# Float16 halves, turned by DMA, for the queries and keys of two of four batches, a sign step on 16-bit words, and a new order

## The chip, the cores and the metric

The kernel runs on one core of one Trainium2 chip. The metric is the time of one execution in microseconds of the device, from launch to the last output; the median of several runs counts. The core has a matrix engine (TensorE, PE; its weight loads are PEld), a vector engine (VectorE, DVE), a scalar engine (ScalarE, ACT), GpSimd (POOL) and a sync engine (SyncE, SP), which issues the transfers here. Each engine works through its own queue in the order of the program; they wait for each other by semaphores.

## The reference

Causal attention over 4 batches, 12 heads, 448 positions and 64 dimensions a head, and behind it a product of gates on the joined heads (1792 rows of 768):

```python
scores = scale * np.matmul(q, k.transpose(0, 1, 3, 2))      # q, k, v: 4 x 12 x 448 x 64, float32
scores = np.where(mask, -1000000000.0, scores)
scores = scores - np.max(scores, axis=-1, keepdims=True)
attn = np.exp(scores)
attn = attn / (np.sum(attn, axis=-1, keepdims=True) + 1e-09)
x = np.matmul(attn, v)                                      # heads joined: 1792 x 768
a = x @ w1                                                  # w1, w2: 768 x 1024, float64
b = x @ w2
h = a * b @ w3                                              # w3: 1024 x 1024
return h @ w_out                                            # w_out: 1024 x 768
```

## The kernel before, in words

**Weights.** The weights come as float64, two 32-bit words a value. `decode` (line 580) makes float32 of them: ScalarE scales the high word and the low word's top bits (L589, L591), DVE shifts the exponent into place (L593) and puts the sign of the high word into the low one (L595, a scalar_tensor_tensor of and and or over all 32-bit words), GpSimd adds the two (L598). There are 40 such steps, 24 of 768 and 16 of 512 columns, all in the first 235 us. w3 and w_out are multiplied to one matrix first, in f32 on PE (L677 turns, L689 products); this product and w1, w2 are then split into two float16 parts, high and remainder, so that later products run as three float16 matmuls (high by high, high by low, low by high).

**Attention.** `pair(p)` (line 439) handles two heads of one batch; there are 24, six to a batch. It loads k and q with 112 rows on partitions (qkr), turns them on PE in f32 (L457, eight turns a pair) and copies them out of PSUM (L461 on ACT or L462 on DVE) into qkt. The first head's 64 dimensions then lie on partitions 0 to 63, the second's on 64 to 127. `scores(u, due)` multiplies q and k in f32: u = 0 to 2 are the first head's row blocks with 128, 256 and 384 columns, u = 3 to 5 the second's (L495), u = 6 the 64 rows of both tails with 448 columns (L493). In a trace each f32 product is two records. The bank of PSUM that a score block takes is one of four named sc. DVE scales, masks and takes the maximum (L499), ACT takes the exponential (L503), the reciprocal of the sum comes from DVE (L510, L513), and the probabilities are split into two float16 parts (L528, L530 or L532, and L535). A DMA with transpose (L403) turns them into pt and ptt; PE multiplies them with the split v (L556, L561); ACT and DVE write the two parts of x (L570, L571, L573). The scale of v, a power of two, comes from squares summed on ACT (`squares`, L355), a sum over partitions on PE against a tile of ones (`root_scale`, L367) and three small steps on DVE (L370 to L375). `scaled` (L381 to L384) and `remainder` (L390) make the parts.

**Gates and output.** `gate(b)` begins with `norms(b)` (L764), then 16 groups of 18 float16 matmuls of 448 columns (L813 to L815). `project(b)` multiplies with the joined matrix (L873 to L875), and SP sends the result out.

**Order.** Nothing is issued in the order of the code. Every step is put into a list with a due time (`prog.add`), the engines that may do it, and an estimated cost. `Program.order` then runs through the list once, before the kernel exists, and gives each free engine the ready step with the earliest due time; what comes out is the fixed order of every engine's queue. All due times hang on the numbers in PLAN. Before, the estimate for a DVE step of over 0.4 us grows by 0.4 of the time in which GpSimd works beside it.

**Memory.** Buffers are rings: two for qkr and qkt, three for p32 and pt, three for da (decoding and squares). Of the 16 tiles w16 with the parts of w1 and w2, nc = 11 lie in fixed memory; the others lie in memory that is free once the f32 product of w3 and w_out is through (the keys w0 and w5).

Of the kernel before, what the change touches and what calls it, by code (L numbers as in the profile page):

```python
# [26 lines left out]
PLAN = dict(nc=11, wstep=2.3205, soft=49.445, w0=118.4, w34=0.5037, ab=1.5277, out=0.179, gap=16.057, lat=37.703, begin=100.181, wlead=94.567, urgent=13.056, flex=96.023, sc=-27.259, vo=62.311, av=-129.283, x=-15.194, qlead=-18.284, rlead=-5.245, v0=30.056, v1=123.832, gram=2, nf=3, h0=3, hv=5, ns=7, wo0=-132.371, wo1=27.123, wom=21.268, w3a=15.279, w3l=17.856, wd=16.165, wh=-60.261, wl=58.537, fin=8.526, ev=-0.539, po=[-24.2, -29.15, -19.26, 10.49, -17.08, -21.38, -42.72, -39.55, -25.07, -1.21, -22.27, 20.91, 0.72, -56.42, -27.16, -10.64, -22.5, -16.12, -21.26, -21.97, -35.13, 2.64, -7.32, 4.13], wo=[-28.62, 5.45, -16.93, 42.18, 23.33, -12.43, 22.11, -20.21], w3=[-35.5, -43.06, -39.69, 7.92, 8.15, -9.78, -9.89, -29.26], tw=[-16.09, -51.07, -16.26, 0.98, -3.04, -29.34, -21.69, -23.59, -23.52, -22.71, -68.85, 16.04, -16.6, -4.06, -30.21, 7.83], slack=0.7, pflex=42.748)  # L27
# [19 lines left out]
class Program:  # L47
# [3 lines left out]
    def __init__(self):  # L51
        self.ops, self.writer, self.readers = [], {}, {}
        self.banks, self.leased, self.first = {}, [], set()

# [31 lines left out]
    def order(self):  # L86
# [12 lines left out]
        dma_free = 0.0  # L99
# [11 lines left out]
        while len(result) < n:  # L111
# [81 lines left out]
def t_pool(n):  # L193
    return (2.1 * n + 150) / 1000
# [7 lines left out]
def tile_causal_attention_moe(ctx: ExitStack, tc: tile.TileContext, q, k, v, w1, w2, w3, wo, out):  # L202
# [33 lines left out]
    def ring(shape, dt, name, n):  # L236
        return Ring(name, fixed(shape, dt, name, n))
# [40 lines left out]
    qkt = ring([P, 2, S], F32, "qkt", 2)  # L278
# [109 lines left out]
    def remainder(dst, src, s, hi, n, due, reads, writes, stage=None):  # L388

        prog.add(due, (DVE, t_dve(n) + 0.06, lambda: nc.vector.scalar_tensor_tensor(  # L390
            out=dst, in0=src, scalar=s, in1=hi, op0=ALU.mult, op1=ALU.subtract)), reads, writes, stage)
# [47 lines left out]
    def pair(p):  # L439
# [10 lines left out]

        qt, qtk = qkt.next()
        for i in (1, 0):
            ps, key = prog.lease("sc", "tr")

            def turn(i=i, ps=ps):
# [5 lines left out]
                (ACT, t_act(S, True), lambda i=i, ps=ps: nc.scalar.copy(out=qt[:, i], in_=ps[:, :S])),  # L461
                (DVE, t_dve(S), lambda i=i, ps=ps: nc.vector.tensor_copy(qt[:, i], ps[:, :S])),  # L462
            ], [key], [qtk + (i,)])

# [17 lines left out]
        def scores(u, due):  # L482
# [6 lines left out]
            def products():  # L489
                for j in range(2):  # L490
                    rows = slice(j * D, (j + 1) * D)
                    if i == 2:
                        nc.tensor.matmul(ps[rows, :w], qt[rows, 0, 3 * P : S], qt[rows, 1, 0:w], start=True, stop=True)  # L493
                    elif i == j:
                        nc.tensor.matmul(ps[:, :w], qt[rows, 0, c * P : (c + 1) * P], qt[rows, 1, 0:w], start=True, stop=True)  # L495

            prog.add(due, (PE, 0.9 if i == 2 else max(2 * t_mm(w) + 0.1, 0.31), products),
                     [qtk + (1,), qtk + (0,)], [key, tk + (c,)] + ([tk] if p < 2 else []))
            prog.add(due + 0.4, (DVE, t_dve(w) + 0.09, lambda: nc.vector.tensor_tensor_reduce(  # L499
                out=o, in0=ps[:, :w], in1=m, scale=minus, scalar=-NEG,  # L500
                op0=ALU.add, op1=ALU.min, accum_out=mx[:, u : u + 1])),
                [key, "minus", "mask_t" if i == 2 else "mask"], [mk + (u,), tk + (c,)] + ([tk] if p < 2 else []))
# [12 lines left out]
        def soft(i, us, due):  # L515
# [3 lines left out]
            for u in reversed(us):  # L519
# [5 lines left out]
                else:  # L525
# [9 lines left out]
                prog.add(due + 0.4, (DVE, t_dve(w) + 0.06, lambda src=src, r=r, h=h, l=l: nc.vector.scalar_tensor_tensor(  # L535
                    out=l, in0=src, scalar=r, in1=h, op0=ALU.mult, op1=ALU.subtract)),
# [5 lines left out]
        for n, u in enumerate((2, 5, 1, 4, 0, 3, 6)):  # L542
            scores(u, T + PLAN["sc"] + 0.3 * n)
# [37 lines left out]
    def decode(raw, rawk, n, due, t=None, tk=None):  # L581
# [11 lines left out]
        prog.add(due + 1, (DVE, t_dve(n, True), lambda: nc.vector.tensor_scalar(  # L593
            out=ai, in0=ai, scalar1=3, scalar2=None, op0=ALU.logical_shift_left)), [ak], [ak])
# [21 lines left out]
    def take_w(i):  # L616
# [19 lines left out]
        prog.add(T + PLAN["wl"], (DVE, t_dve(DM) + 0.06, lambda: nc.vector.scalar_tensor_tensor(  # L636
# [335 lines left out]
```

## Time and profile before

| what | value |
|---|---|
| median of 3 runs | 641.41 us (641.22 to 641.45) |
| the profiled execution, its own time | 642.41 us |
| its span, first to last instruction | 640.6 us |
| PE, DVE, ACT, POOL busy | 601.3, 405.5, 318.7, 175.0 us |
| mean granted clock of PE | 0.974 |
| PE's share of the chain that ended last | 74%, DVE 14%, issue 5% |
| DMA | 78.29 MB, 54.3% of 16 engines' span |
| start of norms for gates 0 to 3 (L764) | 208, 318, 443, 549 us |
| tail scores of pairs 12, 18 and 23 (L493) | 296, 417, 523 us |

A line of the profile names the source line, the engine, the operation and the tiles, then count, busy time and mean. PE is pipelined: the time of one matmul runs on under the next, so what a matmul costs is read from the start of one to the start of the next. The granted clock is a share of full speed; 1.00 is 2.4 GHz, and means between 0.5 and 1 are mixtures of the two levels, 1.2 and 2.4 GHz.

### The profile page before, as it was taken

Reading aid. Unit: us, or ns where it says so; the run is one execution under the profiler, and the core shown is the slowest. Engines: PE = TensorE matmul, PEld = TensorE weight load, DVE = VectorE, ACT = ScalarE, POOL = GpSimd, SP = SyncE. Lnnn points to the kernel's source line nnn. Section 1 sums busy time; section 2 is a strip of 40 time slices with the busy share of each in tenths; the row PEclk is TensorE's granted clock in tenths of the full one; section 3 lists DMA queues with packets and bytes.
Section 4 is the critical chain, followed back from the end, with each engine's and each line's share of the span. In section 5 each row is a group of like instructions: output and inputs, shape, how many; then the busy total and the mean of one; then the engine's idle time right before and its main releaser. Section 6 shows DMA issues by size and latency. Waiting matters only on the chain.

```text
span 640.6 us, 10699 instructions
## 1 busy us (share of the span) xinstructions
PE 601.3 (94%) x3892; PEld 342.3 (53%) x3892; DVE 405.5 (63%) x1048; ACT 318.7 (50%) x739; POOL 175.0 (27%) x129
## 2 busy tenths in 40 slices
PE   3799969987989999999999999999999999999997
PEld 1454545655545555565655556555555556555564
DVE  7966999999989889866543358846528861212200
ACT  7546988587666867446331336635425441111111
POOL 5643754641554524313100023311102210000000
PEclk9899978988889999999999999999999999999999
DMA  8899596464888949759610139797107616000011
GB/s 340 248 235 226 130 235 169 133 186 111 162 153 170 189 103 154 129 102 185 141 30 19 40 76 176 152 172 143 29 2 150 125 23 124 26 1 1 0 50 49
DMA packets 198836, 78.29 MB, mean 122 GB/s; under 512 B 179840, under 2 KB 195712, under 8 KB 198784
## 3 DMA queue, kind: packets, MB, share of 16 engines
q1 hardware_dynamic: 198784, 77.61, 54.3%
q8 instruction: 30, 0.49, 0.3%
q14 instruction: 22, 0.18, 0.1%
HBM read 43.78 MB, written 5.51 MB: 77 GB/s over the span
## 4 chain that ended last, share of the span: by engine, by line
PE 74%; DVE 14%; issue 5%; ACT 4%; DMA 2%; POOL 0%; SPq 0%; DVEq 0%; ACTq 0%; POOLq 0%
PE sc L495 8%; PE mm L813 7%; PE mm L814 7%; PE mm L815 7%; PE mm L873 4%; PE mm L875 4%; PE mm L874 4%; PE mm L689 3%; PE tr L813 3%; PE tr L814 3%; PE tr L815 3%; PE av L561 3%; PE sc L493 3%; PE sc L689 2%; PE sc L457 2%
## 5 line engine op out<-in xcount | busy, mean ns | idle before, releaser
L532 POOL TENSOR_SCALAR ph<-p,rc 128x256 f16<-128x256 f32 (+2 forms) x47 | 52.8, 1128 | 162.2 <-DVE rc L513 66.4
L814 PE MATMUL mm<-xt,w 128*128 128x448 f16 x258 | 91.4, 354 | 1.9 <-DVE xt L573 1.9
L813 PE MATMUL mm<-xt,w 128*128 128x448 f16 x258 | 91.6, 355 | 0.4 <-ACT xt L570 0.2
L815 PE MATMUL mm<-xt,w 128*128 128x448 f16 x258 | 91.6, 355 | 0.0
L503 ACT ACTIVATE p<-p,mx 128x384 f32<-128x384 f32 (+2 forms) x144 | 71.7, 499 | 37.9 <-DVE mx L499 37.7
L499 DVE CUSTOM_DVE_ANT_0 p<-sc,mask,minus 128x384 f32<-128x384 f32 (+2 forms) x144 | 64.0, 480 | 30.6 <-PE sc L495 29.9
L495 PE MATMUL sc<-qkt 64*128 64x384 f32 (+2 forms) x288 | 72.8, 415 | 5.2 <-DVE mx L499 2.7
L689 PE MATMUL mm<-wof,w3t 128*128 128x384 f32 x192 | 73.3, 522 | 3.5 <-POOL wof L598 3.5
L535 DVE SCALAR_TENSOR_TENSOR ph<-p,rc,ph 128x384 f16<-128x384 f32 (+2 forms) x144 | 67.1, 509 | 3.6 <-ACT ph L530 2.3
L495 PEld LDWEIGHTS sc<-qkt 64*128 64x128 f32 x288 | 41.5, 190 | 40.3 <-issue 9.7
L813 PEld LDWEIGHTS <-w 128*128 128x128 f16 x384 | 38.2, 100 | 38.4 <-issue 5.5
L815 PEld LDWEIGHTS <-w 128*128 128x128 f16 x384 | 37.7, 98 | 38.0 <-issue 3.5
L814 PEld LDWEIGHTS <-w 128*128 128x128 f16 x384 | 37.8, 98 | 30.8 <-issue 1.1
L689 PEld LDWEIGHTS mm<-wof,w3t 128*128 128x128 f32 x192 | 36.6, 203 | 25.8 <-issue 4.7
L873 PE MATMUL mm<-w34h,arena 128*128 128x384 f16 x152 | 49.8, 327 | 0.0
L875 PE MATMUL mm<-w34h,arena 128*128 128x384 f16 x152 | 49.5, 326 | 0.0
L874 PE MATMUL mm<-w34l,arena 128*128 128x384 f16 x152 | 49.5, 326 | 0.0
L813 PE MATMUL tr<-xt,w 128*128 128x448 f16 x126 | 44.9, 357 | 0.0
L814 PE MATMUL tr<-xt,w 128*128 128x448 f16 x126 | 44.9, 356 | 0.0
L815 PE MATMUL tr<-xt,w 128*128 128x448 f16 x126 | 44.9, 356 | 0.0
L839 ACT CAST arena<-g 128x448 f16<-128x448 f32 x21 | 11.8, 564 | 57.4 <-DVE g L834 57.3
L834 DVE SCALAR_TENSOR_TENSOR g<-mm,y,at 128x448 f32<-128x448 f32 x17 | 11.6, 684 | 42.0 <-PE mm L815 41.8
(165 smaller groups left out, 1097.6 us busy)
## 6 DMA issues: line engine op xcount, KB each, us to landing
arena<-in_moe_w_dram SPq DMA_DIRECT2D x11, 768.0 KB, 4.7
qkr<-in_k_dram SPq DMA_DIRECT2D x24, 224.0 KB, 4.0
qkr<-in_q_dram SPq DMA_DIRECT2D x24, 224.0 KB, 4.7
vr<-in_v_dram SPq DMA_DIRECT2D x24, 192.0 KB, 4.3
out_dram<-osb SPq DMA_DIRECT2D x24, 192.0 KB, 2.0
arena<-in_moe_w_dram SPq DMA_DIRECT2D x8, 512.0 KB, 4.4
xt<-in_moe_w_dram SPq DMA_DIRECT2D x5, 768.0 KB, 4.7
arena<-in_moe_w_out_dram SPq DMA_DIRECT2D x3, 768.0 KB, 6.7
```

Of the source, the lines that this page charges most:

```text
L495: nc.tensor.matmul(ps[:, :w], qt[rows, 0, c * P : (c + 1) * P], qt[rows, 1, 0:w], start=True, stop=True)
L499: prog.add(due + 0.4, (DVE, t_dve(w) + 0.09, lambda: nc.vector.tensor_tensor_reduce(out=o, in0=ps[:, :w], in1=m, scale=minus, scalar=-NEG, ...
L503: prog.add(due + 0.9, (ACT, t_act(w, pointers=1, acc=True), lambda: nc.scalar.activation(out=o, in_=o, func=AF.Exp, scale=-1.0, bias=mx[:, ...
L532: (POOL, t_pool(w) + 0.35e-3 * w + 0.16, lambda src=src, r=r, h=h: nc.gpsimd.tensor_scalar(out=h, in0=src, scalar1=r, scalar2=None, op0=AL ...
L535: prog.add(due + 0.4, (DVE, t_dve(w) + 0.06, lambda src=src, r=r, h=h, l=l: nc.vector.scalar_tensor_tensor(out=l, in0=src, scalar=r, in1=h ...
L689: prog.add(due, (PE, 4 * t_mm(NH), lambda: nc.tensor.matmul(ps[:, :NH], w3t[slot(m)][:, g], wof[:, g, ns], start=g == 0, stop=g == KF - 1) ...
L813: nc.tensor.matmul(ps[:, :S], w[:, 0, d], xh, start=d == 0, stop=False)
L814: nc.tensor.matmul(ps[:, :S], w[:, 0, d], xl, start=False, stop=False)
L815: nc.tensor.matmul(ps[:, :S], w[:, 1, d], xh, start=False, stop=d == KD - 1)
L873: nc.tensor.matmul(t, gh[:, fc, cs], w34h[:, fc, ns], start=fc == 0, stop=False)
L874: nc.tensor.matmul(t, gh[:, fc, cs], w34l[:, fc, ns], start=False, stop=False)
L875: nc.tensor.matmul(t, gl[:, fc, cs], w34h[:, fc, ns], start=False, stop=fc == KF - 1)
```

## The change

Three things. **First**, the pairs of batches 2 and 3 (b >= PLAN["fq"] = 2) no longer go through PE's f32 turns. `halved` loads q and k in their natural layout (three loads each, 256-byte rows), finds a power of two as a scale for each, as v has one (squares on ACT, a sum on PE, three steps on DVE), splits each into a float16 high part and remainder, and has a DMA turn both parts at once (8 blocks of 128 by 128). The scores of these pairs are three float16 passes, each a step of its own in the list, with due times that put the two heads' passes side by side. The scale goes out again in DVE's step at L499 (scale=iv in place of minus). GpSimd clears the unused rows of the two qkr buffers once. Batches 0 and 1 keep the old way, as `turned_whole`. **Second**, the sign step takes the top 16-bit word of the high word, keeps its top bit and writes it as the top 16-bit word of the low word; the low word's value has three bits, so nothing is lost. **Third**, the estimate of DVE beside GpSimd counts only marked steps, and all numbers of PLAN are new, nc among them (10 for 11).

```diff
@@ Program.order @@
-                if e == DVE and cost > 0.4:
-                    cost += 0.4 * max(0.0, min(free[POOL], t + cost) - t)
+                if e == DVE and emit in self.shared:
+                    cost += 0.9 * max(0.0, min(port, t + cost + 1.0) - t)
+                    port_dve = t + cost
+                if e == POOL and emit in self.pairs:
+                    cost += 0.6 * max(0.0, min(port_dve, t + cost) - t)
+                    port = t + cost
...
+    def halved(p, b, hs, T, qk, qkk, qt, qtk):
+
+        q16 = qt.rearrange("p i f -> p (i f)").bitcast(F16).rearrange("p (i t f) -> p i t f", i=2, t=2)
+        inverse_of = []
+        for i, src in ((1, k), (0, q)):
...
+            squares(am, flat, lambda n16=n16: n16[:, 1].bitcast(BF16), 4 * P, T - PLAN["hlead"], raw_k, [ak, nk])
+            sc_, sck, e, ek = root_scale([am], [ak], "q", T - PLAN["hlead"])
+            inverse_of.append((e, ek))
+            scaled(n16[:, 0], flat, sc_, 4 * P, T - PLAN["hlead"] + 0.5, raw_k + [sck], [nk])
+            remainder(n16[:, 1], flat, sc_, n16[:, 0], 4 * P, T - PLAN["hlead"] + 1, raw_k + [sck, nk], [nk])
+            dma(q16[:, i].rearrange("p t (c f) -> p (t c) f", f=P), n16.rearrange("p t f -> p (t f)"), T - PLAN["hlead"] + 1.5,
+                [nk], [qtk + (i,)], P * P * 2 * 8, turn=True)
...
+        halves = b >= PLAN["fq"]
...
+            if halves:
+                q16 = qt.rearrange("p i f -> p (i f)").bitcast(F16).rearrange("p (i t f) -> p i t f", i=2, t=2)
+                for m_, (a, b_) in enumerate(((0, 0), (0, 1), (1, 0))):
+                    prog.add(due + 0.01 * m_, (PE, t_mm(w) / (1 if i == 2 else 2) + 0.02, lambda a=a, b_=b_, m_=m_: products(
+                        q16[:, 0, a], q16[:, 1, b_], m_ == 0, m_ == 2)),
+                        [qtk + (1,), qtk + (0,)], [key, tk + (c,)] + ([tk] if p < 2 else []))
...
-            scores(u, T + PLAN["sc"] + 0.3 * n)
+            scores(u, T + PLAN["sc"] + 0.3 * (2 * (n // 2) if halves else n) + 0.001 * n)
...
+        parts16 = raw.rearrange("p n t -> p (n t)").bitcast(I16).rearrange("p (n t) -> p n t", t=4)
...
-        prog.add(due + 1, (DVE, t_dve(n) + 0.06, lambda: nc.vector.scalar_tensor_tensor(
-            out=raw[:, :, 0], in0=raw[:, :, 1], scalar=-0x80000000, in1=raw[:, :, 0], op0=ALU.bitwise_and, op1=ALU.bitwise_or)),
+        prog.add(due + 1, (DVE, 0.9 if n > 512 else 0.65, lambda: nc.vector.tensor_scalar(
+            out=parts16[:, :, 1], in0=parts16[:, :, 3], scalar1=-0x8000, scalar2=None, op0=ALU.bitwise_and)),
             rawk + [low], [low])
-        prog.add(due + 2, (POOL, t_pool(n) + 0.2, lambda: nc.gpsimd.tensor_tensor(
-            out=t.bitcast(I32), in0=ai, in1=raw[:, :, 0], op=ALU.add)), rawk + [ak, low], tk)
+        prog.add(due + 2, (POOL, t_pool(n) + 0.1, prog.alone(lambda: nc.gpsimd.tensor_tensor(
+            out=t.bitcast(I32), in0=ai, in1=raw[:, :, 0], op=ALU.add))), rawk + [ak, low], tk)
...
```

## Rows read from the trace of the kernel before

**Rows 1.** The page, busy tenths in 40 slices, PE and DVE

```profile
PE   3799969987989999999999999999999999999997
DVE  7966999999989889866543358846528861212200
```

**Rows 2.** By stage: PE, PEld, DVE, ACT, POOL busy, granted clock, DMA share, GB/s

```profile
0.00:80.00 80.00, 64.98 (x226) 35.16 (x226) 62.29 (x112) 53.14 (x106) 44.22 (x39) 0.98 0.85 235
80.00:160.00 80.00, 68.80 (x283) 42.91 (x282) 74.34 (x150) 61.66 (x116) 37.75 (x20) 0.88 0.59 167
160.00:240.00 80.00, 73.46 (x576) 42.40 (x577) 73.15 (x208) 54.49 (x135) 36.42 (x24) 0.95 0.81 155
...
320.00:440.00 120.00, 119.15 (x858) 66.65 (x857) 64.47 (x197) 49.81 (x136) 21.03 (x18) 1.00 0.51 101
440.00:560.00 120.00, 119.16 (x906) 67.42 (x904) 63.78 (x190) 44.22 (x111) 14.12 (x12) 1.00 0.35 71
```

**Rows 3.** The same table for lines 495, 493, 457 alone (PE, PEld)

```profile
320.00:560.00 240.00, 25.91 (x120) 14.52 (x120) 1.00 0.43 86
...
320.00:560.00 240.00, 9.69 (x40) 1.94 (x40) 1.00 0.43 86
...
320.00:560.00 240.00, 9.97 (x80) 8.61 (x80) 1.00 0.43 86
```

**Rows 4.** PE in order of time: both heads' scores, tail, gate (start, us)

```profile
452.30 1.35 PE L495 MATMUL sc<-qkt 64*128 64x384 f32 x8
453.92 0.48 PE L495 MATMUL sc<-qkt 64*128 64x128 f32 x2 [0.28 <-DVE mx L499]
...
455.43 0.97 PE L493 MATMUL sc<-qkt 64*64 64x448 f32 x4
456.33 0.36 PE L813 MATMUL mm<-xt,w 128*128 128x448 f16 x1
456.53 0.35 PE L814 MATMUL mm<-xt,w 128*128 128x448 f16 x1
```

**Rows 5.** The same view: one head's scores, then value products

```profile
388.56 1.56 PE L495 MATMUL sc<-qkt 64*128 64x384 f32 x6
390.06 0.36 PE L813 MATMUL mm<-xt,w 128*128 128x448 f16 x1
...
392.14 1.15 PE L561 MATMUL av<-pt,v 128*64 128x384 f16 x18
393.22 1.12 PE L495 MATMUL sc<-qkt 64*128 64x384 f32 x3
```

**Rows 6.** The same view: the two sums of v's scale

```profile
475.07 0.50 PE L367 MATMUL sc<-vam,ones 128*128 128x1 f32 x4
475.43 0.35 PE L813 MATMUL mm<-xt,w 128*128 128x448 f16 x1
```

**Rows 7.** Busy DVE by stage, the sign step (line 595) alone

```profile
0.00:80.00 80.00, 32.51 (x21) 0.98 0.85 235
80.00:160.00 80.00, 16.44 (x16) 0.88 0.59 167
160.00:240.00 80.00, 4.20 (x3) 0.95 0.81 155
```

**Rows 8.** One line's DVE instructions: ns min/median/max, first and last start

```profile
L595 DVE SCALAR_TENSOR_TENSOR arena<-arena x22: 680/948/2591, 5.7 to 230.4; 128x768 int32<-128x768 int32 x14, 128x512 int32<-128x512 int32 x8
...
L593 DVE TENSOR_SCALAR da<-da x38: 385/550/2211, 5.2 to 231.4; 128x768 int32<-128x768 int32 x24, 128x512 int32<-128x512 int32 x14
...
L390 DVE SCALAR_TENSOR_TENSOR v<-vr,v_s,v x24: 736/746/992, 153.9 to 524.8; 128x512 f16<-128x512 f32 x24
```

**Rows 9.** PE's waits by line up to 250 us: total, times, longest

```profile
PE sc L367 <- ACT w L355: 7.0, 4, 2.7
```

**Rows 10.** The tail tile's turn by DMA: SP's queue, time to landing

```profile
L403 SPq DMA_TRANSPOSE ptt<-pht x24: 1233/1736/2013, 77.5 to 534.5; - x24
...
DMA to landing us min/median/max: 3.0/3.6/6.0
```

More of the change, by code (lines that the diff above doesn't have):

```diff
@@ L53, in __init__, with beside, alone @@
         self.banks, self.leased, self.first = {}, [], set()
+        self.shared, self.pairs = set(), set()
+    def beside(self, emit):
+        self.shared.add(emit)
+        return emit
+    def alone(self, emit):
+        self.pairs.add(emit)
+        return emit
     def lease(self, *pools):
@@ L388, in remainder @@
     def remainder(dst, src, s, hi, n, due, reads, writes, stage=None):
-        prog.add(due, (DVE, t_dve(n) + 0.06, lambda: nc.vector.scalar_tensor_tensor(
-            out=dst, in0=src, scalar=s, in1=hi, op0=ALU.mult, op1=ALU.subtract)), reads, writes, stage)
+        prog.add(due, (DVE, t_dve(n) + 0.06, prog.beside(lambda: nc.vector.scalar_tensor_tensor(
+            out=dst, in0=src, scalar=s, in1=hi, op0=ALU.mult, op1=ALU.subtract))), reads, writes, stage)
     def less(dst, a, b, n, due, reads, writes):
@@ L437, in tile_causal_attention_moe, with turned_whole, turn @@
     UP = 2.0**14
+    def turned_whole(p, b, hs, T, qk, qkk, qt, qtk):
+        for i, src in ((1, k), (0, q)):
+            dma(qk[0:QP, i], src[b, hs].rearrange("h (p r) d -> p r h d", r=4),
+                T - PLAN["qlead"], (), [qkk + (i,)], 2 * S * D * 4, rate=181e3)
+        for i in (1, 0):
+            ps, key = prog.lease("sc", "tr")
+            def turn(i=i, ps=ps):
+                for r in range(4):
+                    nc.tensor.transpose(ps[:, r:S:4], qk[0:QP, i, r].rearrange("p h d -> p (h d)"), ident[0:QP, 0:QP])
+            prog.add(T + 0.1 * (1 - i), (PE, 4 * t_mm(2 * QP), turn), [qkk + (i,)], [key, qtk + (i,)])
+            prog.add(T + 0.5, [
+                (ACT, t_act(S, True), lambda i=i, ps=ps: nc.scalar.copy(out=qt[:, i, :S], in_=ps[:, :S])),
+                (DVE, t_dve(S), lambda i=i, ps=ps: nc.vector.tensor_copy(qt[:, i, :S], ps[:, :S])),
+            ], [key], [qtk + (i,)])
+        return minus, "minus"
@@ L439, in pair, with clear_pads @@
+    def clear_pads(due):
+        for n, t in enumerate(qk_raw.tiles):
+            kk = ("qkr", n)
+            prog.add(due, (POOL, 0.4, lambda t=t: nc.gpsimd.memset(t[D:P, :, 3], 0.0)), [], [kk + (i, *n) for i in range(2) for n in ((), (0,), (1,), (2,))])
     def pair(p):
@@ L445, in pair @@
         hs = slice(2 * hp, 2 * hp + 2)
[L446 to L448 removed]
+        halves = b >= PLAN["fq"]
         qt, qtk = qkt.next()
[L452 to L463 removed]
+        load = halved if halves else turned_whole
+        iv, ivk = load(p, b, hs, T, qk, qkk, qt, qtk)
         vs, vsk, _, _ = vsc[b]
@@ L487, in scores, with products @@
             m = mask_t if i == 2 else mask[:, (2 - c) * P :]
-            def products():
+            n = min(P, S - c * P)
+            def products(qs, ks, start, stop):
                 for j in range(2):
                     rows = slice(j * D, (j + 1) * D)
[L492 to L495, printed above, removed]
@@ L635, in take_w @@
         ], tk + [sk] + w5, [("w16h", i)])
-        prog.add(T + PLAN["wl"], (DVE, t_dve(DM) + 0.06, lambda: nc.vector.scalar_tensor_tensor(
-            out=w16[i][:, 1], in0=tc2, scalar=s, in1=w16[i][:, 0], op0=ALU.mult, op1=ALU.subtract)),
+        prog.add(T + PLAN["wl"], (DVE, t_dve(DM) + 0.06, prog.beside(lambda: nc.vector.scalar_tensor_tensor(
+            out=w16[i][:, 1], in0=tc2, scalar=s, in1=w16[i][:, 0], op0=ALU.mult, op1=ALU.subtract))),
             tk + [sk, ("w16h", i)] + w5, [("w16l", i)])
```

52 lines of the change are left out of this document (34 added, 18 removed).

## The prediction

> **What bounds the kernel now.** I read the page's row of slices first [rows 1], then the table by stage [rows 2], then what each stage's engines do by line. Two regimes show. From 240 us on, TensorE (PE) has no room: 119.15 of 120 us busy in each of the two late windows, at the full granted clock, while VectorE (DVE) works 64.47 and 63.78 of 120 [rows 2]. There a microsecond of matmul taken away is a microsecond of time, as long as no new wait appears. Before 240 us it is the other way round: between 80 and 240 DVE is busy 74.34 and 73.15 of 80, PE 68.80 and 73.46 of 80, and the granted clock is 0.88 and 0.95, part of it at the lower level, because PE idles [rows 2]. There DVE's load decides more than PE's. The change touches both: float16 scores act on the late stage (batches 2 and 3, pairs 12 to 23, whose tail tiles start at 296 us by the table above), the sign step on the first 240 us, the new order on all.
>
> **Scores of the last two batches: what goes.** The window from 320 to 560 us holds the score work of ten pairs (40 records of L493, four to a pair). In it PE is busy 25.91 us with the six f32 products of 128 to 384 columns (L495), 9.69 us with the tail tile (L493) and 9.97 us with the eight f32 turns (L457) [rows 3]: 4.56 us a pair. A block's last matmul drains under the next block's first (the L493 block counts 0.97 us, but the next matmul starts 0.90 us after it, 455.43 to 456.33 [rows 4]), so I take off 0.25 us for the blocks' ends: 4.3 us a pair go.
>
> **What comes in its place on PE.** (a) The six products in three float16 passes. No float16 score stands in the trace, but the value products have the same columns: three passes of 384, 256 and 128 columns for two heads side by side, 18 matmuls, 392.14 to 393.22, 1.08 us [rows 5]. That is the price if the two heads' products, which stand in different halves of the array's rows, run at the same time; if not, twice that, 2.16 us. (b) The tail tile: three passes of 448 columns, two halves at once, at 0.20 us a step (456.33 to 456.53 [rows 4]), and 0.1 us for the way in and out: 0.7 us. (c) Two sums over partitions, for the scale of q and of k: the v scale's two sums cost 0.36 us (475.07 to 475.43 [rows 6]). (d) A wait for a score bank: only four exist. Where both heads run at once PE already waits 0.28 us for DVE before the 128-column product [rows 4]; the float16 products fill the four banks some 0.4 us earlier, DVE empties them no faster, so I add 0.3 us, and 0 as the other end where the order puts gate matmuls between.
>
> Do the heads run at once? In f32 they do where the order put them beside each other: 384 and 256 columns of both heads take 452.30 to about 453.6, 1.35 us, eight records [rows 4]; one head's 384, 256 and 128 alone take 1.49 us, 388.56 to 390.06 [rows 5]. Blocks of the first kind number seven between 330 and 520 us, so somewhat more than half of the pairs. The new due times put heads 2 and 5, 1 and 4, 0 and 3 within a thousandth of each other, pass by pass, so I take eight of twelve. Paired: 1.08 + 0.7 + 0.36 + 0.3 = 2.4, a saving of 1.9 us; unpaired: 2.16 + 0.7 + 0.36 = 3.2, a saving of 1.1. Eight and four: 19.6 us.
>
> A rule of the Trainium skill speaks against counting on that. Its page "TensorEngine Tiling (Array Packing)", section "Key Properties", says that different tiles run in parallel, but also that changing the tiling mode, not just the tile, drains TensorE. The trace agrees in sign and sizes it: the way into and out of a score block costs about 0.1 us each. By that rule every pass that stands alone among gate matmuls would pay both ways; it is the first rival below.
>
> (e) Waits. The change puts three new things ahead of PE's in-order queue: the sum waits for ScalarE's squares, the scores wait for the turned halves. The only row of such a sum is L367 behind L355: 7.0 us in four waits [rows 9]; over the 28 sums of weights and v in that kernel that is 0.25 us each, and 24 new sums would cost 6 us. Ends 0 and 6; I take 1.5, because those waits fell where ScalarE and DVE were crowded. Behind a waiting sum stand the gate and output matmuls, and behind those everything. Late term: 19.6 - 1.5 = **18 us**, ends 7 (all unpaired, full waits) and 26 (all paired, no bank wait).
>
> **The rest of the float16 path** I cost at nothing, with its cover named. DVE gets two remainders of 512 columns at 0.75 us [rows 8] and seven small operations a pair, about 2.5 us, 30 us for twelve pairs; it loses the few turned-tile copies that fell to it. DVE has about 56 us of 120 free in each late window [rows 2], so it goes from 53% to some 70%: hidden unless it bunches up in front of a score bank. ScalarE loses two copies and gains two squares and up to two scalings; it has more room than DVE. On SP's queue come four more loads and two turns a pair. The nearest row is the turn of the tail tile, of the same size: 1.74 us of SP's queue, 3.6 us to landing, 6.0 at the worst [rows 10]. These pass in front of the probability turns on the same queue; the cover is that q and k have two buffers, so a pair's halves may be made a pair ahead. If that cover is gone, see the slower rival.
>
> **Sign step.** L595 is 32.51, 16.44 and 4.20 us of DVE in the first three windows, 53.2 us for 40 instructions [rows 7], though one takes 0.68 us at the least and 0.95 at the median; the worst took 2.59 [rows 8]: part of it is time lost beside GpSimd. The new operation reads one source and half the bytes. The costs written in the diff are 0.9 us for 768 columns and 0.65 for 512; by them 24 and 16 instructions take 32 us: 21 us less. Ends: the old operation undisturbed, about 0.95 and 0.68, 34 us (19 less), and the trace's one-source shift on tiles of the same width (L593, median 0.55 us [rows 8]), 22 us (31 less). I take 21: 16.4 of it in the first 80 us, 4.8 between 80 and 240. What is that worth in time? In the first 80 us loads, start-up and PE's f32 products limit as well (PE busy 64.98 of 80, DMA share 0.85 [rows 2]), so little comes straight out; in the DVE-bound stretch 4.8 come straight out, and something of the 16.4 if softmax work is pulled forward. Ends 0 and 20 (PE idles about 18 us between 80 and 240, and the low clock hides some more). I take **7 us**.
>
> **Order and tiles.** All due times are new, with a finer price for DVE beside GpSimd. The trace can't price an order; I give it 0 with 5 us either way. One w16 tile fewer lies ahead of the point where the first stage's memory is given back; gate 0 asks for it only after ten groups of 18 matmuls at 0.19 us, some 34 us in, so it costs nothing unless that point slips.
>
> **Sum.** 642.41 us of the profiled execution (span 640.60 and 1.81 around it) less 18 and 7 is 617.4. The median of the runs lies 1.0 us under the profiled one, so the forecast is 616.4 us.
>
> **Rivals.**
> First, the passes scatter: heads unpaired and half of the passes single among gate matmuls. Then a pair saves 1.1 us less about 0.6 for three extra blocks at 0.2: 6 us for twelve pairs; with 4 us early, 632 profiled, 631 us. For: score work is now three program steps per product, each free to be put elsewhere. Against: each pass is ready the moment the one before ends, and the due times differ by hundredths. Chance 0.17.
> Second, the first third is really DVE's: all 20 us of the early end come out, with 21 late: 601 profiled, 600 us. For: DVE at 92% from 80 to 240 [rows 2]. Against: most of the sign step lies before 80 us [rows 7]. Chance 0.13.
> Third, slower: SP's queue. Two turns a pair at 1.74 us each [rows 10] stand in an in-order queue in front of the probability turns and of the next pair's loads. If they pass through to PE, twelve pairs cost 12 x 3.5 = 42 us against 25 saved: 659 us. It decides from 25/12, about 2.1 us of PE wait a pair, and such waits would lower the clock too. For: the turn needs the longest new chain (load, squares, sum, scale, remainder, turn). Against: PE's only wait for such work today is in [rows 9], and queue time of two turns is small against some 20 us a pair. Chance 0.10.
> Fourth, it doesn't do what it says: DVE's added 30 us delay the gate's products, and PE's saved time becomes waits for banks: no change, 641. Chance 0.03.
>
> **How the numbers follow.** Forecast case 0.50 (608 to 624 by its own ends), first rival 0.17 (626 to 638), second 0.13, third 0.10, fourth 0.03; 0.07 for weaker mixtures between 633 and 640. A difference under 0.2%, 1.3 us, can't be told from no change in this kernel. Faster: 0.50 + 0.17 + 0.13 + 0.07 = 0.87; same 0.03; slower 0.10. The range of 602 to 637 leaves out about half of the second rival, the slower ones and a little of the mixtures, 0.2 in all.
>
> **What would show it.** Right: in the late windows PE still above 99% busy; no turns by L457 after the third batch begins; float16 score blocks of both heads near 1.1 us a pair, starts a few ns apart; the last gate's norms (549 us in the table above) some 22 us sooner; L595 near 0.9 and 0.65 us; norms of gate 0 (208 us there) some 7 us sooner. Wrong: PE idle behind the new sums or the new turns, score steps alone between gate matmuls, the clock under 1.00 after 240 us, or a gate 0 that starts no earlier with DVE less busy.

## The result, and the profile after

| | median us | range | against before |
|---|---|---|---|
| before | 641.32 | 638.58 to 641.45 | |
| after | 625.08 | 624.77 to 625.31 | 0.9761 (0.9735 to 0.9786) |

The change takes 16.2 us off, where 25 were forecast; the time lies inside the range. The profiled span went from 640.6 to 623.3 us.

The page of the kernel after: TensorE's (PE's) busy time, then busy tenths of PE and VectorE (DVE) and the granted clock in 40 slices.

```profile
PE 586.3 (94%) x3940; PEld 327.7 (53%) x3940; DVE 428.0 (69%) x1155; ACT 331.2 (53%) x781; POOL 189.4 (30%) x138
...
PE   2999974999989899999999999999999999999997
...
DVE  6977879799999878985666775597697853212100
...
PEclk9999985899999799999999999999999999999999
```

PE has 15.0 us less to do (601.3 before). Its slices stay at 9 from some 218 us on, where they did from some 192 us in [rows 1]; DVE's late slices are fuller. By stage (columns as in [rows 2]):

```profile
0.00:80.00 80.00, 66.28 (x230) 35.24 (x231) 64.67 (x123) 53.20 (x103) 42.04 (x37) 1.00 0.95 248
80.00:160.00 80.00, 66.56 (x293) 40.16 (x293) 70.81 (x143) 58.96 (x113) 45.27 (x25) 0.85 0.64 167
160.00:240.00 80.00, 74.67 (x552) 43.09 (x549) 70.52 (x212) 56.68 (x147) 37.53 (x26) 0.94 0.73 146
320.00:440.00 120.00, 120.00 (x963) 65.99 (x964) 88.65 (x291) 63.56 (x176) 25.32 (x21) 1.00 0.71 133
440.00:545.00 105.00, 105.00 (x850) 58.35 (x849) 65.08 (x200) 45.58 (x118) 16.63 (x14) 1.00 0.51 99
```

Two things are to be seen. In the late stage PE is at 100% and at the full clock, with DVE at 88.65 of 120: the halved path's extra DVE work is hidden. In the first 240 us PE is busy 207.5 us in sum, against 207.2 by [rows 2]: nothing came out there, although DVE is less busy between 80 and 240. The norms of gates 0 to 3 now start at 213.2, 314.4, 430.5 and 531.8 us: gate 0 is 5 us later, the last one 17.2 us sooner. All of the gain arises behind gate 0.

Where it went is told best by PE's time from the start of each matmul to the start of the next, idle time taken out, added up over the whole trace by what is computed. The last three columns belong to experiments told of below.

| PE, us | before | after | halves alone | no halves | halves, two due times |
|---|---|---|---|---|---|
| f32 scores | 91.1 | 52.4 | 49.7 | 91.0 | 51.6 |
| float16 scores | 0 | 25.8 | 27.6 | 0 | 28.4 |
| f32 turns of q, k | 20.5 | 11.8 | 11.9 | 20.7 | 10.6 |
| sums for their scales | 0 | 4.5 | 5.1 | 0 | 4.8 |
| *score path, sum of the four* | 111.6 | 94.6 | 94.3 | 111.7 | 95.4 |
| gates | 224.4 | 223.9 | 227.9 | 223.3 | 226.1 |
| all other matmuls | 265.1 | 267.5 | 265.9 | 266.1 | 266.7 |
| PE stands still | 27.0 | 24.7 | 41.3 | 26.7 | 23.0 |

The score path is 17.0 us shorter, and the span 17.3. The other rows shift by up to 2.5 us either way and nearly cancel.

One pair's scores in the kernel after, PE in order of time (start, us; the counterpart of [rows 4]):

```profile
452.21 0.99 PE L550 MATMUL sc<-qkt 64*128 64x384 f16 x12
453.13 0.36 PE L878 MATMUL mm<-xt,w 128*128 128x448 f16 x1
453.33 0.35 PE L879 MATMUL mm<-xt,w 128*128 128x448 f16 x1
453.52 0.35 PE L880 MATMUL mm<-xt,w 128*128 128x448 f16 x1
453.81 0.34 PE L550 MATMUL sc<-qkt 64*128 64x128 f16 x3
454.08 0.36 PE L878 MATMUL mm<-xt,w 128*128 128x448 f16 x1
...
454.75 1.02 PE L550 MATMUL sc<-qkt 64*128 64x128 f16 x9
455.70 0.36 PE L878 MATMUL mm<-xt,w 128*128 128x448 f16 x1
```

The first block holds 12 matmuls, the 384 and the 256 columns of both heads: the second head's start 3 to 4 ns after the first's, and the next matmul follows 0.92 us after the first. The 128 columns come head by head (0.27 us to the next gate matmul; the last group holds the other head's and the tail). Between them stand gate matmuls, and no float16 score waits for a bank. PE's only wait for another engine after 240 us is this one, at 274 us, in front of an f32 score of the second batch (PE's waits by line: total, times, longest):

```profile
PE sc L550 <- DVE mx L563: 0.3, 1, 0.3
```

The sign step (L660, DVE, the stages of [rows 7]) and its instructions (ns min/median/max):

```profile
0.00:80.00 80.00, 28.22 (x21) 1.00 0.95 248
80.00:160.00 80.00, 16.16 (x17) 0.85 0.64 167
160.00:240.00 80.00, 2.08 (x2) 0.94 0.73 146
...
L660 DVE TENSOR_SCALAR arena<-arena x22: 735/1024/2386, 5.8 to 237.1; 128x768 int16<-128x768 int16 x14, 128x512 int16<-128x512 int16 x8
```

It is 46.5 us for 53.2, not 32, and its median is longer than the old one's, 1024 ns against 948 in [rows 8].

### The profile page after: what moved, and what is told of

It is laid out like the page before. It is cut to its first block, busy times and chain, and to the rows that moved or that the text cites. A ratio compares the mean times of both kernels' runs of the same rounds, so it can differ in the third digit from the quotient of the medians.

```text
span 623.3 us, 11048 instructions
## 1 busy us (share of the span) xinstructions
PE 586.3 (94%) x3940; PEld 327.7 (53%) x3940; DVE 428.0 (69%) x1155; ACT 331.2 (53%) x781; POOL 189.4 (30%) x138
## 4 chain that ended last, share of the span: by engine, by line
PE 82%; DVE 8%; DMA 4%; ACT 3%; issue 2%; POOL 1%; SPq 0%; DVEq 0%; ACTq 0%; POOLq 0%
PE sc L550 11%; PE mm L878 9%; PE mm L879 8%; PE mm L880 8%; PE mm L754 6%; PE mm L938 4%; PE mm L940 4%; PE mm L939 4%; PE av L625 4%; PE tr L878 4%; PE tr L880 4%; PE tr L879 4%; PE tr L938 2%; PE av L620 2%; PE tr L939 2%; PE tr L940 2%
## 5 line engine op out<-in xcount | busy, mean ns | idle before, releaser
L878 PE MATMUL mm<-xt,w 128*128 128x448 f16 x264 | 93.5, 354 | 0.0
L879 PE MATMUL mm<-xt,w 128*128 128x448 f16 x264 | 93.1, 353 | 0.0
L880 PE MATMUL mm<-xt,w 128*128 128x448 f16 x264 | 93.1, 353 | 0.0
L567 ACT ACTIVATE p<-p,mx 128x384 f32<-128x384 f32 (+1 forms) x144 | 71.6, 498 | 31.9 <-DVE mx L563 31.1
L550 PE MATMUL sc<-qkt 64*128 64x384 f16 (+6 forms) x480 | 84.7, 367 | 2.1 <-DVE mx L563 1.9
L599 DVE SCALAR_TENSOR_TENSOR ph<-p,rc,ph 128x384 f16<-128x384 f32 (+2 forms) x144 | 72.6, 546 | 0.2
L879 PEld LDWEIGHTS <-w 128*128 128x128 f16 x384 | 37.6, 98 | 28.7 <-issue 0.6
L938 PE MATMUL mm<-w34h,arena 128*128 128x384 f16 x152 | 49.7, 327 | 0.0
L878 PE MATMUL tr<-xt,w 128*128 128x448 f16 x120 | 42.5, 354 | 0.1
L880 PE MATMUL tr<-xt,w 128*128 128x448 f16 x120 | 42.3, 353 | 0.0
L879 PE MATMUL tr<-xt,w 128*128 128x448 f16 x120 | 42.3, 353 | 0.0
L563 DVE CUSTOM_DVE_ANT_0 p<-sc,mask,minus 128x256 f32<-128x256 f32 (+2 forms) x72 | 33.2, 477 | 12.3 <-PE sc L550 11.9
L550 PEld LDWEIGHTS sc<-qkt 64*128 64x128 f32 (+1 forms) x192 | 24.3, 178 | 25.7 <-issue 9.2
L563 DVE CUSTOM_DVE_ANT_0 p<-sc,mask,qiv 128x384 f32<-128x384 f32 (+2 forms) x72 | 30.9, 480 | 10.0 <-PE sc L550 9.7
```

Of the source, the lines that this page charges most:

```text
L550: nc.tensor.matmul(ps[rows if i == 2 else slice(0, P), :w], qs[rows, c * P : c * P + n], ks[rows, 0:w], start=start, stop=stop)
L567: prog.add(due + 0.9, (ACT, t_act(w, pointers=1, acc=True), lambda: nc.scalar.activation(out=o, in_=o, func=AF.Exp, scale=-1.0, bias=mx[:, ...
L599: prog.add(due + 0.4, (DVE, t_dve(w) + 0.06, prog.beside(lambda src=src, r=r, h=h, l=l: nc.vector.scalar_tensor_tensor(out=l, in0=src, sca ...
L878: nc.tensor.matmul(ps[:, :S], w[:, 0, d], xh, start=d == 0, stop=False)
L879: nc.tensor.matmul(ps[:, :S], w[:, 0, d], xl, start=False, stop=False)
L880: nc.tensor.matmul(ps[:, :S], w[:, 1, d], xh, start=False, stop=d == KD - 1)
```

## Experiments

Ratios are to the kernel before, run on the same chip; 0.001 is 0.64 us. The four of the first group tell the parts apart.

**The sign step alone**: before, with its 16-bit form and the same queues.

```diff
-        ... scalar_tensor_tensor(out=raw[:, :, 0], in0=raw[:, :, 1], scalar=-0x80000000, in1=raw[:, :, 0], ...)
+        ... tensor_scalar(out=parts16[:, :, 1], in0=parts16[:, :, 3], scalar1=-0x8000, ..., op0=ALU.bitwise_and)
```

> The kernel before with the sign step on 16-bit words alone; the planned costs are left as they were, so every engine's queue has the same order. Theory A (the operation itself saves nothing: alone it takes 1.03 us for 768 columns in the changed kernel against 0.95 before, and both stand still behind a two-tensor add of GpSimd that has begun): 641 us, within 1.5, and L595's total stays within 50 to 56 us. Rival B (the 16-bit step gives back its 5 to 7 us of DVE and the new order lost them again): 634 to 637 us.

Measured: 639.94 us, ratio 0.9994 (0.998 to 1.0009). The step takes 53.6 us of DVE for 40 instructions, as before (53.2). Its instructions:

```profile
L596 DVE TENSOR_SCALAR arena<-arena x22: 727/1031/2691, 5.8 to 228.5; 128x768 int16<-128x768 int16 x14, 128x512 int16<-128x512 int16 x8
```

So with the order held fixed the step carries nothing, in DVE time or in the end.

**The old sign step in the new order**: after, with line 660 put back.

```diff
-        ... tensor_scalar(out=parts16[:, :, 1], in0=parts16[:, :, 3], scalar1=-0x8000, ...)
+        ... scalar_tensor_tensor(out=raw[:, :, 0], in0=raw[:, :, 1], scalar=-0x80000000, in1=raw[:, :, 0], ...)
```

> The changed kernel with the old sign step (both 32-bit words, two tensors) under the same planned costs, so the order is that of the changed kernel. Theory A: 625 us, within 1.5, a shade quicker if anything. Rival B: 629 to 632 us, since the changed order would then carry 7 us more of DVE work before 240 us.

Measured: 623.85 us, ratio 0.9756 (0.9731 to 0.978), not told apart from after. The old step took 42.7 us here, less than the new one in the same order. That the total went from 53.2 to 46.5 between before and after is the order's doing: of the 40 instructions, 15 took over 0.6 us more than their time alone in before and 12 with the new step in before's order, but 7 in after and 6 here.

**The halves alone**: before's due times and estimates, with the halved path for batches 2 and 3. The halving's own due time, hlead, is that of the new plan.

```diff
-PLAN = dict(nc=11, ..., pflex=42.748)
+PLAN = dict(nc=11, ..., pflex=42.748, fq=2, hlead=-11.33)
+    def halved(p, b, hs, T, qk, qkk, qt, qtk):
...
```

> The kernel before with the float16 path for batches 2 and 3 alone: old sign step, old plan numbers and old cost rule, only the due times of the new steps added; its first third is ordered as before. Theory A (the float16 scores carry the whole gain, about 1.75 us of PE a pair, 21 us in all, and the new order lost some 4 us before 240 us): 619 to 624 us, gate 0 at 208 us. Rival C (the due times made for it carry a good part; with the old ones PE waits for the turned halves): 630 us or more, with PE idle behind the turns or the new sums.

Measured: 645.87 us, ratio 1.0103 (1.0073 to 1.0133): slower by 1%. The table above tells why. The score path is 17.3 us shorter, just as in after; PE stands still 14.3 us more, and gates and the other matmuls cost 4.3 us more, most of it in the stretches where the granted clock is at its lower level. Windows around the gaps (columns as above), then PE's waits from 240 us on:

```profile
420.00:440.00 20.00, 13.35 (x154) 7.03 (x150) 16.84 (x58) 11.32 (x37) 7.05 (x5) 0.91 0.87 150
440.00:460.00 20.00, 18.03 (x99) 10.22 (x100) 9.99 (x32) 7.95 (x16) 1.03 (x1) 0.83 0.93 155
540.00:560.00 20.00, 11.59 (x110) 7.18 (x110) 8.20 (x28) 6.14 (x19) 2.12 (x2) 0.76 0.36 69
```

```profile
PE av L616 <- DMA ptt<-pht: 9.9, 3, 8.4
PE sc L378 <- ACT da L366: 3.6, 2, 2.1
PE tr L874 <- DVE xt L633: 2.8, 1, 2.8
```

The chain of waits around the largest gap, in order of time (start, us, what):

```profile
540.04 0.64 PE sc L546 x6
540.68 0.61 DVE p L559
...
541.33 3.06 ACT p L563 x12
...
544.63 0.20 DVE rc L573
...
546.27 1.82 issue
548.09 0.68 ACT pht L590
548.76 2.92 SPq L414
...
551.78 3.06 DMA ptt<-pht
...
554.88 0.85 PE av L616 x23
```

From the last scores at 540.0 to the value products at 554.9 the chain takes 15 us, through softmax, SP's queue and the transfer. PE has run out of gate and output matmuls at 546.5 and stands for 8.4 us. In the kernel before, the same chain was covered: the last pair's scores start at 519.4 and the value products at 539.8 us, with no wait of PE in front of them (PE in order of time, before):

```profile
519.45 1.35 PE L495 MATMUL sc<-qkt 64*128 64x384 f32 x8
...
539.75 0.57 PE L556 MATMUL av<-ptt,v 128*64 128x64 f16 x24
```

So the chains of the halved pairs do not start sooner with less work ahead of them. Eleven of the twelve start later than in the kernel before: the tail scores of pairs 12, 18, 19 and 23 start at 320.7, 435.0, 473.7 and 542.8 us, where the f32 ones stood at 296.4, 417.3, 438.3 and 523.1. One reason can be read from the kernel: `halved` takes two of the three buffers da for each pair, in turn with the squares of the next v (both call `da.next()`). By this turn pair 19, the second of batch 3, comes behind that batch's v, and the trace shows it so (ScalarE, SP's queue and PE, start and us):

```profile
456.04 1.48 ACT L366 ACTIVATE da<-vr 128x1536 bf16<-128x1536 f32 x1 [0.29 <-DMA vr<-in_v_dram]
457.53 0.61 ACT L366 ACTIVATE da<-qkr 128x512 bf16<-128x512 f32 x1
...
458.14 0.61 ACT L366 ACTIVATE da<-qkr 128x512 bf16<-128x512 f32 x1
...
464.20 1.26 SPq L414 DMA_TRANSPOSE qkt<-da  x1
470.09 0.99 PE L546 MATMUL sc<-qkt 64*128 64x384 f16 x12
```

The squares of the v run first, those of two halves right behind them, then one turn and the pair's scores. No run gave the ring a fourth buffer, so how much of the delay is the ring's and how much the due times' is not shown.

**The order and the sign step without the halves**: after, with all batches on the old path.

```diff
-PLAN = dict(nc=10, ..., fq=2, hlead=-11.33)
+PLAN = dict(nc=10, ..., fq=4, hlead=-11.33)
```

> The changed kernel with f32 turns and f32 scores in all batches: sign step, plan numbers and cost rule of the change without the float16 path. Theory A: 642 to 648 us, gate 0 near 213 us as in the changed kernel, late stage as slow as before. Rival C: 630 to 636 us.

Measured: 642.33 us, ratio 1.0038 (1.002 to 1.0057). PE is busy 601.3 us, as before. So the new order and the sign step are worth nothing (a little less than nothing) without the halves, and the halves lose in the old order. Only together do they gain.

**Are all the new due times needed?** In the halves-alone kernel I changed one number, the due time of the loading, squares and scale of v of the next batches; then a second, hlead, the due time of the halving, which is not a number of the old plan.

```diff
-PLAN = dict(..., v1=123.832, ..., fq=2, hlead=-11.33)
+PLAN = dict(..., v1=98.15, ..., fq=2, hlead=-11.33)
```

> The run of the float16 path alone on the old plan gave 645.9 us, with PE idle 8.8 us at 546 us and 9 us around 430 behind turned probabilities that came late. This kernel is that one with one number changed: the next batch's v is loaded and scaled earlier (v1 98.15 for 123.83). Theory E (the pairs' chains start too late for the shorter matmul time, and PE runs out of gate and output matmuls before them): the idle around 430 us goes, that at 546 us shrinks; 622 to 632 us. Rival F (the turns by DMA themselves are too slow, whatever the due times): 642 us or more.

```diff
-PLAN = dict(..., v1=98.15, ..., fq=2, hlead=-11.33)
+PLAN = dict(..., v1=98.15, ..., fq=2, hlead=45)
```

> The same with a second number: the halves of q and k are made earlier (hlead 45 for -11.33). The first third keeps the order of the kernel before but for the place of one v load, the sign step is the old one. Theory E: PE is full from 240 us to the end, gate 0 stays near 206 us against 213 in the changed kernel, so 616 to 621 us, under both kernels. Rival F: 640 us or more. Rival C (only the new plan as a whole carries it): 628 us or more.

Measured: 627.19 us, ratio 0.9791 (0.9757 to 0.9825), with v1 alone; 625.23, 0.9745 (0.9711 to 0.978), with both. The sum for batch 3's v, which stood at 464.2 us with the halves alone, stands at 448.4 with v1 changed, and the scores of that batch's second pair start at 456.9 instead of 470.1, those of the last pair at 524.3 instead of 540.0. One gap of 3.4 us is left, again in front of the value products of the tail, at 537 us; with the second number it goes, and the last pair's scores start at 509.3. The same three windows of the kernel with both:

```profile
420.00:440.00 20.00, 20.00 (x165) 11.56 (x165) 11.74 (x38) 8.91 (x24) 1.94 (x2) 1.00 0.84 162
440.00:460.00 20.00, 20.00 (x153) 10.94 (x150) 11.50 (x39) 10.08 (x23) 0.55 (x1) 1.00 0.46 91
540.00:560.00 20.00, 20.00 (x107) 10.37 (x106) 3.92 (x6) 3.29 (x6) 0.00 (x0) 1.00 0.00 1
```

PE is full again and the clock is back (the expected 616 to 621 us did not come; gate 0's norms start at 210.2 us, not near 206), with the same turns by DMA on the same queue. The old plan with two due times changed, one of its own and the halving's, gives all that the new plan gives.

**Only the late due times**: the last kernel, but v earlier for batches 2 and 3 alone, so that the old first third stays.

```diff
-PLAN = dict(..., v1=98.15, ..., fq=2, hlead=45)
+PLAN = dict(..., v1=123.832, ..., fq=2, hlead=45)
-                take_v(2, p // 3 - 2, starts[p] + PLAN["v1"])
+                take_v(2, p // 3 - 2, starts[p] + 85)
...
-                        take_v(b + 2, p // 3 % 2, starts[p] + PLAN["v1"])
+                        take_v(b + 2, p // 3 % 2, starts[p] + 85)
```

> The float16 path on the old plan, old sign step and old cost rule, with the halves made earlier (hlead 45) and the v of batches 2 and 3 loaded earlier (85 for 123.83), while batch 1's v keeps its old due time, so the first third is ordered as in the kernel before. Theory E: gate 0 at 205 to 208 us as in the kernel before (213 in the changed one), PE full after it; 619 to 622 us, some 4 us under the changed kernel. Rival C (the new plan as a whole carries the rest): 625 us or more.

Measured: 623.73 us, ratio 0.9744 (0.9727 to 0.9761), not told apart from after. Gate 0's norms start at 206.5 us, 6.7 sooner than in after, without an earlier end: its float16 scores cost 28.7 us for 25.8, since the heads met less often. When gate 0 starts is a matter of order; it is no measure of what the first third costs.

**The two heads' passes apart**: after, with each head's products due 0.3 us after the one before, and no pairing.

```diff
-            scores(u, T + PLAN["sc"] + 0.3 * (2 * (n // 2) if halves else n) + 0.001 * n)
+            scores(u, T + PLAN["sc"] + 0.3 * n)
```

> The changed kernel with one edit: the score steps of the float16 pairs get due times 0.3 apart in turn, as the f32 ones have, so the two heads' passes no longer stand beside each other. In the changed kernel the 384- and 256-column passes of both heads run at once, 0.94 us a pair together. Theory A (pairing is a real price on PE): without it they cost about 0.8 us more a pair, 9 to 10 us for twelve pairs, 632 to 636 us, and PE stays full. Rival D (heads overlap anyway, or DVE's pace at the score banks sets the pace): 625 us, within 1.5.

Measured: 627.72 us, ratio 0.9793 (0.9769 to 0.9818), some 2 us over after. The program now lists one head's three passes of 384 columns before the other's, yet they ran side by side all the same, 10 ns apart instead of 4. A block of this kernel, PE in order of time:

```profile
384.28 0.99 PE L550 MATMUL sc<-qkt 64*128 64x384 f16 x12
385.20 0.38 PE L382 MATMUL tr<-qam,ones 128*128 128x1 f32 x2
```

Twelve matmuls in 0.92 us again. All float16 scores cost 25.9 us (25.8 in after); the 2 us are short gaps, 2.5 us more of them after 240 us: 1.0 in front of float16 scores that wait for a bank, the rest in front of gate matmuls. The 632 us of theory A did not come. So the pairing did not hang on the new due times to the thousandth; it needs only that the two heads' blocks stand next to each other.

**The turn in two pieces**: after, with each turn of q or k issued as two of half the size, in the same place.

```diff
-            dma(q16[:, i]..., n16..., T - PLAN["hlead"] + 1.5, ..., turn=True)
+            def both(i=i, n16=n16):
+                for t in range(2):
+                    nc.sync.dma_start(out=q16[:, i, t]..., in_=n16[:, t], transpose=True)
```

> The changed kernel in the same order, with each DMA turn of the halves of q and k issued as two (high part, remainder) with the same bytes in all. Theory A (the turns are hidden, each pair's halves are made ahead): 625 us, within 1.5, PE full after 240 us. Rival G (SP's queue is near its limit, the forecast's third rival): 24 more issues at about 1.3 us of SP's queue each reach PE, 630 us or more.

Measured: 626.07 us, ratio 0.9782 (0.9761 to 0.9803). The turns on SP's queue (ns min/median/max), of after and then of this kernel:

```profile
L418 SPq DMA_TRANSPOSE qkt<-da x24: 1232/1274/2018, 289.2 to 503.7; - x24
```

```profile
L496 SPq DMA_TRANSPOSE qkt<-da x48: 1188/1220/2471, 287.3 to 505.3; - x48
```

A piece takes SP as long as the whole. So 24 pieces more put some 28 us on SP's queue, and the end moves by 1 to 1.5 us, with intervals that overlap (0.9761 to 0.9803, and 0.9735 to 0.9786 for after): not told apart. The queue is not what PE waits for.

**The sign step made short**: after, with the step on 32 columns in the same place in all queues (the time of the rest of its columns is left out).

```diff
-            out=parts16[:, :, 1], in0=parts16[:, :, 3], scalar1=-0x8000, ...
+            out=parts16[:, :32, 1], in0=parts16[:, :32, 3], scalar1=-0x8000, ...
```

> The changed kernel, in the same order, with the sign step on the first 32 columns of each weight tile alone, so that weights keep their sign only there; what is left out is DVE work, from 46.5 us to perhaps 8. It measures what DVE time before 240 us is worth. Theory A (the first third is held by loads, GpSimd's adds and the f32 products as much as by DVE): gate 0 at most 5 us sooner, 619 to 624 us. Rival B (the first third is DVE's, as the forecast took a third of the DVE time freed): 38 us less DVE give 12 us or more, 613 us or less.

Measured: 619.96 us, ratio 0.9674 (0.9651 to 0.9696). Its instructions:

```profile
L660 DVE TENSOR_SCALAR arena<-arena x22: 185/203/1840, 5.9 to 231.6; 128x32 int16<-128x32 int16 x22
```

The step falls from 46.5 to 16.8 us, and 29.7 us of DVE give 5.1 to 5.6 us of time: 0.17 to 0.19 per microsecond. Even 32 columns can take 1840 ns, which is no work but standing still.

**What it stands behind.** In after, around 26 us (GpSimd and DVE in order of time):

```profile
25.49 2.09 POOL L663 TENSOR_TENSOR wof<-da,arena 128x768 int32<-128x768 int32 x1 [0.51 <-DVE da L658]
25.80 2.68 DVE L660 TENSOR_SCALAR xt<-xt 128x768 int16<-128x768 int16 x1
...
28.27 1.07 DVE L660 TENSOR_SCALAR w34l<-w34l 128x768 int16<-128x768 int16 x1
...
28.56 2.34 POOL L663 TENSOR_TENSOR wof<-da,xt 128x768 int32<-128x768 int32 x1 [0.98 <-DVE xt L660]
```

The step that starts 0.31 us into GpSimd's add takes 2.68 us: the 1.78 that are left of the add, and 0.9 of its own. The next one, which starts ahead of GpSimd's next add, takes 1.07; here it is the add, which starts while the step runs, that is held up: 2.34 us, where the shortest of its size takes 1.83. To see whether the add's second operand does it, I let GpSimd make its result from one operand (the low word's part is left out of the sum).

```diff
-            ... nc.gpsimd.tensor_tensor(out=t.bitcast(I32), in0=ai, in1=raw[:, :, 0], op=ALU.add)
+            ... nc.gpsimd.tensor_scalar(out=t, in0=a, scalar1=1.0, scalar2=None, op0=ALU.mult)
```

> The changed kernel in the same order, with GpSimd's add of the weights' two words replaced by a pass over one of them, so that the low bits and the sign are left out of the weights. Theory A (what holds the sign step and the shift up is a GpSimd operation that reads two tensors and has begun before them): the sign step then takes 1.03 and 0.74 us nearly everywhere, 36 to 38 us in all against 46.5, the shift about 20 us against 31.7, and gate 0 comes 2 to 5 us sooner: 619 to 624 us. Rival H (any GpSimd work beside them slows them): the sign step stays above 44 us.

Measured: 620.06 us, ratio 0.9689 (0.9663 to 0.9716). The sign step:

```profile
L660 DVE TENSOR_SCALAR arena<-arena x22: 727/1024/1548, 5.8 to 232.6; 128x768 int16<-128x768 int16 x14, 128x512 int16<-128x512 int16 x8
```

On these tiles the longest falls from 2386 to 1548 ns, over all tiles from 2.68 to 1.65 us, the step's sum from 46.5 to 41.9, the shift's (L658) from 31.7 to 24.3. The long standstills are gone, but a 768-column step beside GpSimd still takes 1.24 us on the mean against 1.04 alone. This lies between the two expectations. GpSimd's own step is not shorter for it: its 40 take 87.3 us instead of 68.8, so DVE is beside it more often and yet loses less. The edit also changed the operation and its type (a float32 product for an integer add), so that the number of operands alone makes the difference is likely, not shown.

## Why the prediction was right, and where it was not

**The scores (18 us): right, by its own steps.** Step for step, for a pair, from the starts of the matmuls of all twelve pairs:

| a pair, us | forecast | measured |
|---|---|---|
| goes: f32 products, tail and turns, with 0.14 of waits for a bank | 4.3 | 4.35 |
| three float16 passes, paired | 1.08 | 1.47 |
| tail | 0.7 | 0.69 |
| two sums | 0.36 | 0.38 |
| wait for a bank | 0.3 | 0 |
| comes, paired | 2.4 | 2.53 |

The passes cost more than [rows 5] because the 128-column blocks came head by head, and the bank wait is not there for the same reason: gate matmuls stand between. The heads met in all twelve pairs for 384 columns and in eleven for 256, not in eight, so the pairs gave 21.9 us where 19.6 stood. The new waits, 1.5 us in the sum, did not come; PE waits for no sum and no turn after 240 us. Against that, matmuls elsewhere cost 5.7 us more than before, which the sum did not hold: the f32 scores of the first two batches 2.3, their turns 0.9, the value products 1.2, the turns of w3 0.8, the product of w3 and w_out 0.4. The granted clock between 80 and 160 us is 0.85 now and was 0.88; no run separates what the clock and what the neighbours did here. 21.9 less 5.7, and 1.1 gained in the gates and in gaps elsewhere, is the span's 17.3. That it comes so near to 18 is in part luck: the pairs gave more than forecast, and other matmuls took it back.

**The cover held in the new order.** DVE went to 88.65 of 120 us (64.47 in [rows 2]) and nothing waits for it. SP's queue hid the turns: issuing them twice costs 1 to 1.5 us by the medians, so the third rival, the queue, falls by its price. The first rival, scattered passes, falls too: the heads meet even where the due times part them. The rule that the prediction cites from the Trainium skill, page "TensorEngine Tiling (Array Packing)", section "Key Properties", that a change of the tiling mode drains TensorE, did not become a large price either. In the trace a score block starts 0.29 us after the last gate matmul (453.52 to 453.81), where gate matmuls follow each other in 0.19, so the way in is still about 0.1 us.

**The order (0, 5 either way): the step that was wrong without showing.** I summed the parts as if each had a value of its own. Without the halves, the order and the sign step cost 2.4 us, inside the bound. But the 18 us of the scores were not to be had in the old order: there they are all given back, 14.3 us as idle PE and 4.3 as slower matmuls. Halves alone against after, 645.9 to 625.1, the order carries some 20 us. Parts that need each other can't be summed; the fourth rival, no change at all, would have been closer than the forecast had the order not been made for the halves.

The step that failed is the cover under which I put the rest of the float16 path at nothing: two buffers for q and k, so that a pair's halves may be made a pair ahead. In the old order they came late; the last pair's scores started 20 us later than in the kernel before. The sum left out that the halves take da buffers in turn with v, and that their due time has to be set. What I had named as the slower case, probability turns that reach PE late and lower the clock, is what happened there, but not by SP's queue: the same turns on the same queue leave no gap once v1 and hlead are changed. So the score term was right for this kernel because its due times already stood early enough, which the prediction had not shown.

**The sign step (7 us): wrong, nothing came.** Two of its numbers failed. First the price: I took 0.9 and 0.65 us from the costs written in the diff. Alone, outside the neighbourhood of GpSimd, the step takes 1.03 and 0.74 us against 0.95 and 0.69 for the old one; one source and half the bytes save nothing. And the time lost beside GpSimd, which I had expected to go with the second source, stayed: with the order held fixed the sum is 53.6 us against 53.2. My lower end, 19 us less, was thus not an end. The nearest evidence stood in [rows 8] and was left unread: the shift has one source too, and its longest took 2.2 us, four times its median. A one-source step is not safe from the standstill. Second the exchange: I gave 7 us of time for 21 of DVE, 0.33; measured on 29.7 us, it is 0.17 to 0.19. At that rate even the hoped-for 21 us would have brought some 4 (an estimate). The second rival, a first third bound by DVE alone, falls by the same run.

The page "SBUF — State Buffer" of the Trainium skill, section "Summary: rules for kernel authors", says that where DVE runs in its two-port mode, or reads two SBUF inputs while the GpSimd operation reads SBUF, the second to issue blocks fully until the first is done. The trace agrees for GpSimd's two-operand add: DVE's step waits its remaining 1.78 us, and an add that starts second is held up too. It agrees less for one-operand work on GpSimd, where the steps take 1.24 us on the mean and are not stopped. The sign step reads one input; whether it runs in the two-port mode no run here shows.

**The difference.** The forecast was 8.7 us too fast: 7 for the sign step, 0.7 for the scores (17.3 for 18, where the pairs gave 3.9 more than the 18, other matmuls lost 5.7 and gates and gaps gained 1.1), and 1.0 because the profiled execution of before lay that much over its median, and that of after, 625.1 us, does not.

## What to carry to other kernels

Where a fixed order keeps a matrix engine full, taking matmuls out gains only if the chains behind them start early enough: compare when each pair's scores start, before and after, look which buffers the new steps share with others, and re-time the chain's head. Here the last pair's scores had moved 20 us back, the chain from them to their value products takes 15 us, and two due times were worth 20 us. An operation's price is to be taken from rows of its own kind and neighbourhood, and a cheaper-looking form with fewer bytes is to be timed alone before it is summed. Time freed on an engine that shares a stage's limit can be worth far less than itself (0.17 to 0.19 here); making one step short in place, with all queues as they are, measures it directly.

## What the hardware showed that was not expected

- A DVE step with one operand stands still behind a GpSimd two-operand add that started earlier: 2.68 us for 0.9 of work, and 1.84 us for 32 columns. With a one-operand product on GpSimd the longest is 1.65 us. An add that starts behind a DVE step is held up as well: 2.34 us for 1.83.
- A DVE step over 16-bit words that lie 8 bytes apart takes 1.03 us for 768 of them and 0.74 for 512, more than the two-source step over 32-bit words (0.95 and 0.69).
- Float16 products of 64 rows in the two halves of the array run side by side even when the program lists one half's three passes ahead of the other's: 10 ns apart, twelve matmuls in 0.92 us.
- A turn of four blocks takes SP's queue 1.22 us at the median, one of eight 1.27.
